# Joining the last score units of two head pairs in one PSUM region, and another rotation of the regions

## The chip, the cores and the metric

The kernel runs on one core of a Trainium2 chip. The metric is the device time of one launch in microseconds (us), the median of five runs. The core's engines are TensorE (PE, matrix multiply; its weight loads are listed as PEld), ScalarE (ACT, activation functions), VectorE (DVE, elementwise), GpSimd (POOL) and SyncE (SP, which issues most of the DMA transfers here). Each engine works through its own queue in order, and waits on semaphores for the others. Matmul results land in PSUM, which has eight banks of 512 float32 columns in 128 partitions.

## The reference

T5 attention with a relative position bias, and behind it a two-layer MLP with the "snake" activation. The eight batches (B = 8, H = 8 heads, S = 576, D = 64) become 4608 tokens of 512.

```python
scores = scale * np.matmul(q, k.transpose(0, 1, 3, 2))
...
scores = scores + bias.transpose(2, 0, 1)[None, :, :, :]
scores = scores - np.max(scores, axis=-1, keepdims=True)
attn = np.exp(scores)
attn = attn / (np.sum(attn, axis=-1, keepdims=True) + 1e-09)
return np.matmul(attn, v).astype(np.float32)
...
h = x @ w_in
s = np.sin(alpha * h)
g = h + s * s / (alpha + 1e-09)
return (g @ w_out).astype(np.float32)
```

## The kernel before

**Attention.** A batch `t` has four pairs of heads, `p` = 0 to 3. The scores of a pair are kept transposed, keys in the partitions, and come in six *units*. Units 0 to 3 are the four chunks of 128 keys against queries 0 to 511: two matmuls of 512 columns, one for each head of the pair, each on 64 rows of the array. The unit `"t"` (tail) is the last 64 keys of both heads against all 576 queries: two matmuls of 288 columns on the full array. Unit 4 is the four key chunks against the last 64 queries: eight matmuls of 64 columns. A unit fills up to two PSUM banks; ACT takes the exponential of a whole unit in one instruction (line 707) and writes it to the SBUF tile `u` of the pair: 1024 elements per partition for units 0 to 3, 576 for the tail, 512 for unit 4. DVE multiplies the part near the diagonal by the exponential of the bias (lines 732 and 715; far from the diagonal the factor is 1). Then PE multiplies `u` by V (`plan_av`, groups of nine matmuls with 128 queries each: three groups for queries 0 to 383, two for the others). The row sums come along as a 65th column, and DVE divides (lines 786 and 787). From batch 1 on, transposing DMAs bring the result to `xT`.

**MLP.** A block `b` is 512 tokens. MLP-in makes 16 *hidden chunks* `f` of 128 columns, four matmuls of 512 columns each (`plan_moe_in`). ACT takes the sine (line 867), ACT or DVE the square (874, 876), DVE makes `g` (881), which frees the chunk's PSUM bank. MLP-out (`plan_mo`) adds 16 matmuls in one bank for each quarter of the block; ACT or DVE copies the result out (538, 540). Exponential and sine are in different activation tables, so ACT loads a table (line 939) between the attention of a batch and the hidden stage behind it, and back.

**PSUM.** Six of the banks are three regions of two banks, `R0`, `R1`, `R2`. A region holds one score unit, or two hidden chunks. Hidden chunk `f` takes `R{f // 2 % 2}`, so the MLP uses R0 and R1 alone and its last chunks, 14 and 15, lie in R1. In batch 0 the attention uses R0 and R1, and the banks of R2 (`ca`, `cb`) serve attention output and transposes; from batch 1 (`LAG - 1`) on, score units rotate over all three regions. The other two banks, `am0` and `am1`, are shared by attention output and MLP-out, whichever is free first. In the last MLP blocks `ca` and `cb` serve MLP-out too.

**The order.** Nothing of it is left to the hardware: `Plan` is a list scheduler that runs when the kernel is built. Each task names its engines with a cost, its dependencies, a priority and its buffers; `Plan.run` picks the task that can start first (the priority decides within 0.02 us) and emits its instructions, which fixes the order in each engine's queue. MLP-out matmuls are *fill* (`fill`): they have the lowest priority, and their number among the scores of a batch is bounded (`QUOTA`). Changes between matmuls on 64 rows and on the full array are charged (`T_MODE`). In `plan_qk` the units are emitted in *groups* of one or two, one PE task each; the exponentials follow in `plan_ex`. Before, two pairs from batch 1 on have seven groups and twelve units, and a unit's region is its place in the batch's sequence modulo three:

```python
((0, 0), (0, 1)), ((0, 2), (0, 3)), ((0, "t"),), ((0, 4), (1, 0)),
((1, 1), (1, 2)), ((1, "t"),), ((1, 3), (1, 4)),
...
r = seq.index(y) % nreg
```

Batch 0's attention comes first, then block 0's hidden stage, then the attention of batches 1 and 2, and from there on a hidden stage (block `t - 1`) behind the attention of each batch; batch 7 is followed by blocks 6, 7 and 8.

Of the kernel before, what the change touches and what calls it, by code (L numbers as in the profile page):

```python
# [24 lines left out]
def t_act(n):  # L25
    return n / 1200.0 + 0.052
# [150 lines left out]
LAG = 2  # L177
# [34 lines left out]
def kernel(  # L212
# [93 lines left out]
    ubs = [sgl.tile([128, 9 * S], F16, name=f"u{i}") for i in range(3)]  # L306
# [40 lines left out]
    def new_sc(r, n):  # L347
        if r not in regs or regs[r][0] != n:
            if r in regs:
                regs.pop(r)[1].release()  # L350
            open_reg(r, n)
        shape = [128, 512] if n == 1 else [128, 2, 512]
        return regs[r][1].tile(shape, F32, name="sc", tag="sc", bufs=3 - n)
# [96 lines left out]
    def full(out, lhsT, rhs, start, stop):  # L450
        nc.tensor.matmul(out=out, lhsT=lhsT, rhs=rhs, start=start, stop=stop)  # L451
# [78 lines left out]
    plan = Plan()  # L530
# [92 lines left out]
    QW = ((0, 512), (512, 64))  # L623

    def plan_qk(t, deps, tails, first, gate, early):

        us, ubs = [Cell() for _ in range(NP)], [Buf("u") for _ in range(NP)]
        dones = [{} for _ in range(NP)]
        if t < LAG - 1:
            groups = [[(p, i)] for p in range(NP) for i in (0, 1, 2, 3, "t", 4)]  # L630
            nreg = 2
        else:
            groups = [
                [(y + p, i) for y, i in g] for p in range(0, NP, 2) for g in (
                    ((0, 0), (0, 1)), ((0, 2), (0, 3)), ((0, "t"),), ((0, 4), (1, 0)),
                    ((1, 1), (1, 2)), ((1, "t"),), ((1, 3), (1, 4)),
                )
            ]
            nreg = 3
        seq = [y for g in groups for y in g]  # L640
        head, exs = qk_last[:], []
        for gi, g in enumerate(groups):
            scs, bufs = [Cell() for _ in g], []
            for y in g:
                r = seq.index(y) % nreg
                bufs.append([Buf(f"R{r}"), Buf(f"R{r}")])

            def qk(e, gi=gi, g=g, scs=scs):
                if gi == 0:
                    first()  # L650
                    plan.in_qk, plan.used = True, 0
                    plan.quota = QUOTA.get(t, QUOTA_ELSE)
                plan.share = (gi + 1) / len(groups)
                if gi == len(groups) - 1:
                    plan.in_qk = False
                kT, qT = kTs[t % 2], qTs[t % 2]
                for (p, i), sc in zip(g, scs):
                    if i == 0:
                        us[p].v = new_u()
                    sc.v = new_sc(seq.index((p, i)) % nreg, 2)  # L660
                    if i == "t":
                        for z in range(2):
                            full(sc.v[:, z, 0:288], kts[t % 2][:, p, :],
                                 qT[:, p, 288 * z : 288 * z + 288], True, True)
                        continue
                    for y in range(1 if i < 4 else 4):
                        q0, n = QW[i == 4]
                        k0 = 128 * (i if i < 4 else y)
                        for z in range(2):
                            r = slice(64 * z, 64 * z + 64)  # L670
                            full(sc.v[:, z, n * y : n * y + n], kT[r, p, k0 : k0 + 128],
                                 qT[r, p, q0 : q0 + n], True, True)

            def base(y):
                k_ = [x for x in seq if x[0] == y[0]].index(y)
                return PB + 100 * (16 * y[0] + 2 * k_)

            dur = sum(0.25 if i == "t" else 0.15 if i == 4 else 0.225 for _, i in g)
            m = plan.add(
                {"PE": dur}, qk,  # L680
                [d for p, i in g for d in deps[p] + (tails[p] if i == "t" else [])],
                min(base(y) for y in g), after=head + early,
                new=[x for y in bufs for x in y] + [ubs[p] for p, i in g if i == 0],
            )
            m.mode = "f" if g[0][1] == "t" else "r"
            head = [m]
            for y, sc, b in zip(g, scs, bufs):
                exs.append(plan_ex(t, y, sc, b, us[y[0]], ubs[y[0]], m, gate, base(y),
                                   dones[y[0]]))
        qk_last[:] = [m]  # L690
        return us, ubs, dones, exs

    def plan_ex(t, y, sc, b, u, ub, m, gate, base, done):

        p, i = y

        def ex(e):
            uz = u.v[:, 0:8, :].rearrange("p (z c) q -> p z c q", z=2)
            if i == "t":
                o = u.v[:, 8, :].rearrange("p (b q) -> p b q", b=2)  # L700
                x = sc.v[:, :, 0:288]
            elif i < 4:
                o, x = uz[:, :, i, 0:512], sc.v
            else:
                o = uz[:, :, :, 512:576]
                x = sc.v[:, :, 0:256].rearrange("p z (c q) -> p z c q", c=4)
            nc.scalar.activation(out=o, in_=x, func=AF.Exp, scale=0.125)  # L707

        n = 576 if i == "t" else 1024 if i < 4 else 512
        x = plan.add({"ACT": t_act(n)}, ex, [m] + gate, base + 20, use=b + [ub])  # L710
        if i == "t":

            def bh(e):
                io = u.v[:, 8, 384:576]
                nc.vector.tensor_tensor(out=io, in0=io, in1=mh[:, p, 0:192], op=ALU.mult)

            done[(0, 4)] = x
            done[(1, 4)] = plan.add({"DVE": 0.19}, bh, [x], base + 10,
                                     nb=0.0 if t else T_MH[p > 0], use=[ub])
            return x  # L720
        w = 0 if i < 4 else 1
        q0, n = QW[w]
        for cc in [i] if i < 4 else range(4):
            done[(w, cc)] = x
            lo, hi = max(q0, 128 * cc - 128), min(q0 + n, 128 * cc + 256)
            if lo >= hi:
                continue

            def bd(e, cc=cc, lo=lo, hi=hi):
                io = u.v[:, 0:8, lo:hi].rearrange("p (z c) q -> p z c q", z=2)[:, :, cc]  # L730
                x0 = lo - 128 * cc + 128
                nc.vector.tensor_tensor(  # L732
                    out=io, in0=io, in1=m2[:, 2 * p : 2 * p + 2, x0 : x0 + hi - lo],
                    op=ALU.mult,
                )

            done[(w, cc)] = plan.add({"DVE": 0.1 + (hi - lo) / 960.0}, bd, [x], base + 10,
                                     nb=0.0 if t else T_M2[p > 0], use=[ub])
        return x
# [103 lines left out]
    def plan_moe_in(b, tbl):  # L843
# [2 lines left out]
        xs012 = [d for w in range(2) for d in xdone[(0, w)][0 : NP - 1]]  # L846
        xs = [d for t in range(T) for w in range(2) for d in xdone.get((t, w), [])
              if S * t + WIN[w][0] < 512 * b + 512 and S * t + sum(WIN[w]) > 512 * b]
        sins = []
        for f in range(NF):  # L850
            hb, sb, qb = Buf(f"R{f // 2 % 2}"), Buf("s16"), Buf("sq")
            h, s16, sq = Cell(), Cell(), Cell()
# [33 lines left out]
            pri = PB + 10000 + 1000 * (b - (PB // 1000000)) + 10 * f  # L886
            if b == 0 and f < 4:
                m = plan.add({"PE": 3 * t_pe(512)}, lambda e, mm=mm: mm(e, range(3)), xs012,
                             pri - 100, nb=T_W, after=qk_last[:], new=[hb])
                m = plan.add({"PE": t_pe(512)}, lambda e, mm=mm: mm(e, range(3, 4)), xs + [m],  # L890
                             pri, use=[hb])
            else:
                m = plan.add({"PE": 4 * t_pe(512)}, mm, xs, pri, after=qk_last[:] + (exps if b == T - 2 else []),
                             new=[hb])
            x = plan.add({"ACT": t_act(512) + 0.09}, sn, [m, al] + tbl, pri, new=[sb], use=[hb])
            y = plan.add({"ACT": t_act(512) + 0.04, "DVE": 0.34}, sqr, [x], pri - 5,
                         new=[qb], use=[sb])
            gdone[(b, f)] = plan.add({"DVE": t_dve(512)}, gg, [y], pri - 6,
                                     after=[gdone[(b, f - 1)]] if f else [],
                                     new=[gbuf[b]] if f == 0 else [],  # L900
                                     use=[hb, qb] if f == 0 else [hb, qb, gbuf[b]])
# [40 lines left out]
    PB = 0  # L942
    tr = {(0, 0, kq): plan_tr(0, 0, kq, -1000, 0.0) for kq in range(2)}
    al = plan_alpha()
    gate, pe_gate, sins, exps = [], [], [], []

    for t in range(T):
        PB = 1000000 * t
# [12 lines left out]
        if 2 <= t < T - 1:  # L961
            aheads[t + 1] = plan.add({"SP": 0.1}, ahead, [], PB - 1000000,
                                     after=avs[t - 1] + xdone[(t - 1, 1)])
# [5 lines left out]
        sins = []  # L969
        deps, tails = [], []  # L970
# [72 lines left out]
```

## Time and profile before

| | us |
|---|---|
| median of 5 runs | 392.88 (391.96 to 393.08) |
| the profiled execution: its time | 393.21 |
| its span in the trace | 391.4 |
| PE busy / ACT busy / DVE busy | 373.8 / 322.9 / 261.4 |
| first scores of batch 1, first of batch 5 | 54.70, 196.36 |
| hidden stage of batch 5, between its two table loads | 217.65 to 235.24 |
| score stage of batch 6 | 235.24 to 257.65 |
| last matmul ends | about 387.6 |

The span runs from the first to the last instruction of the core; the device time holds some 1.8 us more around it. "Busy" counts the time in which an engine has an instruction at work. Matmuls are pipelined: one of 512 columns is listed with 0.38 us though the next starts 0.2155 us after it, so the work of PE is read from start to start. In a timeline a row merges instructions that follow each other, with its first start, its length and, in brackets, the idle time before it and what ended it. The granted clock is the share of TensorE's full clock.

### The profile page before, as it was taken

The numbers are of one execution on the slowest core, as the hardware profiler recorded it, in microseconds if no ns is written. First come the engines' busy times: TensorE is split into PE (matmuls) and PEld (weight loads), VectorE is DVE, ScalarE is ACT, GpSimd is POOL, SyncE is SP. The second block draws the span as 40 slices with busy tenths as digits, with TensorE's granted clock in tenths as the row PEclk, the third lists the DMA queues.
The fourth block names the chain that finished last, engine by engine and source line by source line (L and its number), as shares of the span: only waits on it lengthen the run. The fifth ranks groups of instructions, "written<-read, shape, count | busy, mean of one in ns | idle before, by whom it ended". The sixth has DMA issues, their size and how long they took to land.

```text
span 391.4 us, 8536 instructions
## 1 busy us (share of the span) xinstructions
PE 373.8 (96%) x3381; PEld 187.6 (48%) x3381; DVE 261.4 (67%) x584; ACT 322.9 (82%) x453; POOL 82.0 (21%) x96
## 2 busy tenths in 40 slices
PE   6789979999999999999999999999999999999995
PEld 2356434555544554455445544454455444444442
DVE  3676976776886679568966786679667949429100
ACT  2966998999999999899999999999999959539211
POOL 5664934062630045005300310000000000000000
PEclk9989989999999999999999999999999999999999
DMA  9999999999999999948992298210121000020122
GB/s 169 206 206 220 169 190 167 160 146 129 148 174 155 147 122 159 186 69 92 139 184 57 32 82 171 79 26 13 54 57 47 16 27 28 28 80 2 58 76 80
DMA packets 151207, 42.58 MB, mean 109 GB/s; under 512 B 140344, under 2 KB 145552, under 8 KB 151168
## 3 DMA queue, kind: packets, MB, share of 16 engines
q0 software_dynamic: 89872, 19.04, 60.2%
q1 hardware_dynamic: 61072, 22.95, 32.8%
q8 instruction: 26, 0.43, 0.5%
q14 instruction: 13, 0.11, 0.1%
q10 hardware_dynamic: 224, 0.05, 0.1%
HBM read 37.76 MB, written 16.52 MB: 139 GB/s over the span
## 4 chain that ended last, share of the span: by engine, by line
PE 87%; DMA 4%; DVE 4%; ACT 3%; POOL 1%; issue 1%; ACTq 0%; DVEq 0%
PE sc L451 42%; PE am L451 37%; PE ca L451 4%; PE cb L451 4%; ACT u L707 2%; DMA m2r<-e_dram 2%; DMA e_dram<-e_sb 1%; DMA phi_sb<-phi_const 1%; DVE g L881 1%; DVE u L732 1%; ACT s L867 1%; DVE xn L787 1%; DVE xp L787 0%; DVE rd L786 0%; DVE outs L540 0%
## 5 line engine op out<-in xcount | busy, mean ns | idle before, releaser
L707 ACT ACTIVATE u<-sc 128x1024 f16<-128x1024 f32 (+1 forms) x192 | 157.8, 892 | 15.2 <-PE sc L451 13.5
L451 PE MATMUL sc<-xT,w_in 128*128 128x512 f16 x576 | 132.4, 379 | 0.5 <-DVE g L881 0.5
L881 DVE SCALAR_TENSOR_TENSOR g<-sq,inv_a,sc 128x512 f16<-128x512 f16 x144 | 103.2, 746 | 24.1 <-PE am L451 16.6
L451 PE MATMUL am<-w_out,g 128*128 128x512 f16 x448 | 116.6, 382 | 0.3 <-DVE outs L540 0.2
L867 ACT ACTIVATE s<-sc,alphaT 128x512 f16<-128x512 f32 x144 | 92.9, 678 | 4.7 <-PE sc L451 3.2
L732 DVE TENSOR_TENSOR u<-u,m2r 128x512 f16<-128x512 f16 (+2 forms) x160 | 68.0, 438 | 32.4 <-ACT u L707 30.2
L451 PEld LDWEIGHTS <-w_in 128*128 128x128 f16 x576 | 55.1, 98 | 64.2 <-issue 1.0
L451 PEld LDWEIGHTS <-g 128*128 128x128 f16 x576 | 53.7, 98 | 66.4 <-issue 12.7
L451 PEld LDWEIGHTS <-u 128*128 128x128 f16 x1440 | 55.9, 98 | 20.0 <-issue 9.5
L451 PE MATMUL am<-v,u 128*128 128x65 f16 x1216 | 53.6, 194 | 0.0
L451 PE MATMUL sc<-qT,kT 64*128 64x64 f16 (+1 forms) x512 | 48.7, 294 | 3.4 <-DVE g L881 2.2
L874 ACT ACTIVATE sq<-s 128x512 f16<-128x512 f16 x79 | 49.2, 628 | 2.5 <-DVE g L881 0.8
L397 POOL DMA_DIRECT2D v<-in_v_dram x24 | 21.2, 893 | 115.4 <-PE am L451 114.2
L451 PE MATMUL am<-vh,u 128*128 128x130 f16 x152 | 33.8, 223 | 2.6 <-DVE xp L787 1.3
L876 DVE TENSOR_TENSOR sq<-s 128x512 f16<-128x512 f16 x65 | 27.3, 421 | 5.1 <-ACT s L867 4.4
L787 DVE TENSOR_TENSOR xp<-am,rd 128x384 f16<-128x384 f32 (+1 forms) x56 | 27.5, 491 | 2.0
L451 PEld LDWEIGHTS <-kT 64*128 64x128 f16 x512 | 14.2, 95 | 29.2 <-issue 25.4
L786 DVE RECIPROCAL rd<-am 128x6 f32<-128x6 f32 (+1 forms) x60 | 11.2, 187 | 22.7 <-PE am L451 22.0
L540 DVE COPY outs<-am 128x512 f32<-128x512 f32 x21 | 14.4, 687 | 6.2 <-PE am L451 6.1
L939 ACT ACT_TABLE_LOAD x13 | 16.7, 1283 | 0.2
L378 POOL DMA_DIRECT2D staged_q<-in_q_dram x6 | 15.0, 2495 | 5.6 <-DMA staged_q<-in_q_dram 3.8
L538 ACT ACTIVATE outs<-am 128x512 f32<-128x512 f32 x7 | 4.2, 594 | 13.6 <-PE am L451 13.6
(87 smaller groups left out, 164.7 us busy)
## 6 DMA issues: line engine op xcount, KB each, us to landing
out_dram<-outs SPq DMA_DIRECT2D x36, 256.0 KB, 2.2
staged_k<-in_k_dram POOLq DMA_DIRECT2D x6, 576.0 KB, 16.8
staged_q<-in_q_dram POOLq DMA_DIRECT2D x6, 576.0 KB, 19.9
v<-in_v_dram POOLq DMA_DIRECT2D x24, 128.0 KB, 8.5
w_in<-in_moe_w_in_dram POOLq DMA_DIRECT2D x4, 512.0 KB, 8.6
w_out<-in_moe_w_out_dram POOLq DMA_DIRECT2D x4, 512.0 KB, 17.5
xT<-xp SPq DMA_TRANSPOSE x72, 3.1
w_out<-in_v_dram SPq DMA_DIRECT2D x4, 256.0 KB, 8.0
```

Source lines behind the costliest of these rows:

```text
L378: nc.gpsimd.dma_start(out=dst.ap()[t].rearrange("s (h d) -> s h d", h=H), in_=src[t].rearrange("h s d -> s h d"),)
L397: nc.gpsimd.dma_start(out=vs[t % 2][:, c, :, 0:D], in_=vp[128 * c : 128 * c + 128],)
L451: nc.tensor.matmul(out=out, lhsT=lhsT, rhs=rhs, start=start, stop=stop)
L540: k_of(e).tensor_copy(out=o, in_=i)
L707: nc.scalar.activation(out=o, in_=x, func=AF.Exp, scale=0.125)
L732: nc.vector.tensor_tensor(out=io, in0=io, in1=m2[:, 2 * p : 2 * p + 2, x0 : x0 + hi - lo], op=ALU.mult,)
L787: nc.vector.tensor_tensor(out=y.rearrange("p c (z d) -> p c z d", z=2), in0=a[:, :, :, 0:D], in1=r.unsqueeze(3).to_broadcast([128, nq, 2, ...
L867: nc.scalar.activation(out=s16.v, in_=h.v, func=AF.Sin, scale=alphaT[:, f : f + 1])
L874: nc.scalar.activation(out=sq.v, in_=s16.v, func=AF.Square)
L876: k_of(e).tensor_tensor(out=sq.v, in0=s16.v, in1=s16.v, op=ALU.mult)
L881: nc.vector.scalar_tensor_tensor(out=gcell[b].v[:, f, :], in0=sq.v, scalar=inv_a[:, f : f + 1], in1=h.v, op0=ALU.mult, op1=ALU.add,)
L939: nc.scalar.preload_act_table_set(name)
```

## The change

From batch 1 on, the unit 4 of two neighbouring pairs becomes one unit `"4"`: sixteen matmuls of 64 columns into one region, the second pair's in columns 256 to 511 of each bank. Two exponentials read it, each for its own pair (`x0` is the column offset). Two pairs then have eleven units, a batch 22 instead of 24, and 13 groups instead of 14; the joined unit stands next to a unit of the following pair, or at the end of the batch behind the last key chunk. The region of a unit is no longer its place modulo three but goes through `order`: R2, R0, R1 in turn, in batch 1 R0, R2, R1 and in batch 2 R2, R1, R0. The priorities of the units of a batch are spread evenly over its sequence. The sines and the squares of a hidden stage are each kept in the order of the chunks (`after=`).

```diff
             groups = [
                 [(y + p, i) for y, i in g] for p in range(0, NP, 2) for g in (
-                    ((0, 0), (0, 1)), ((0, 2), (0, 3)), ((0, "t"),), ((0, 4), (1, 0)),
-                    ((1, 1), (1, 2)), ((1, "t"),), ((1, 3), (1, 4)),
+                    (
+                        ((0, 0), (0, 1)), ((0, 2), (0, 3)), ((0, "t"),), ((1, 0), (1, 1)),
+                        ((1, 2), (1, 3)), ((1, "t"),), ((0, "4"), (2, 0)),
+                    ) if p == 0 else (
+                        ((0, 1), (0, 2)), ((0, "t"),), ((0, 3), (1, 0)), ((1, 1), (1, 2)),
+                        ((1, "t"),), ((1, 3), (0, "4")),
+                    )
                 )
             ]
             nreg = 3
+        order = (0, 1) if nreg == 2 else {LAG - 1: (0, 2, 1), LAG: (2, 1, 0)}.get(t, (2, 0, 1))
...
-                r = seq.index(y) % nreg
+                r = order[seq.index(y) % nreg]
...
-                    for y in range(1 if i < 4 else 4):
-                        q0, n = QW[i == 4]
-                        k0 = 128 * (i if i < 4 else y)
+                    s_ = i in (4, "4")
+                    for y in range(8 if i == "4" else 4 if s_ else 1):
+                        q0, n = QW[s_]
+                        k0, p_ = 128 * (y % 4 if s_ else i), p + y // 4
...
-                            full(sc.v[:, z, n * y : n * y + n], kT[r, p, k0 : k0 + 128],
-                                 qT[r, p, q0 : q0 + n], True, True)
+                            full(sc.v[:, z, n * y : n * y + n], kT[r, p_, k0 : k0 + 128],
+                                 qT[r, p_, q0 : q0 + n], True, True)
...
             def base(y):
+                if t >= LAG - 1:
+                    return PB + 100 * (64 * seq.index(y) // len(seq))
...
-                exs.append(plan_ex(t, y, sc, b, us[y[0]], ubs[y[0]], m, gate, base(y),
-                                   dones[y[0]]))
+                for o in range(2 if y[1] == "4" else 1):
+                    p = y[0] + o
+                    exs.append(plan_ex(t, (p, 4) if y[1] == "4" else y, sc, b, us[p], ubs[p], m,
+                                       gate, base(y) + o, dones[p], 256 * o))
...
-                x = sc.v[:, :, 0:256].rearrange("p z (c q) -> p z c q", c=4)
+                x = sc.v[:, :, x0 : x0 + 256].rearrange("p z (c q) -> p z c q", c=4)
...
-            x = plan.add({"ACT": t_act(512) + 0.09}, sn, [m, al] + tbl, pri, new=[sb], use=[hb])
+            x = plan.add({"ACT": t_act(512) + 0.09}, sn, [m, al] + tbl, pri, after=sins[-1:],
+                         new=[sb], use=[hb])
             y = plan.add({"ACT": t_act(512) + 0.04, "DVE": 0.34}, sqr, [x], pri - 5,
-                         new=[qb], use=[sb])
+                         after=sqs[-1:], new=[qb], use=[sb])
+            sqs.append(y)
```

More of the change, by code (lines that the diff above doesn't have):

```diff
@@ L659, in qk @@
                         us[p].v = new_u()
-                    sc.v = new_sc(seq.index((p, i)) % nreg, 2)
+                    sc.v = new_sc(order[seq.index((p, i)) % nreg], 2)
                     if i == "t":
@@ L665, in qk @@
                         continue
-                    for y in range(1 if i < 4 else 4):
-                        q0, n = QW[i == 4]
-                        k0 = 128 * (i if i < 4 else y)
+                    s_ = i in (4, "4")
+                    for y in range(8 if i == "4" else 4 if s_ else 1):
+                        q0, n = QW[s_]
+                        k0, p_ = 128 * (y % 4 if s_ else i), p + y // 4
                         for z in range(2):
                             r = slice(64 * z, 64 * z + 64)
-                            full(sc.v[:, z, n * y : n * y + n], kT[r, p, k0 : k0 + 128],
-                                 qT[r, p, q0 : q0 + n], True, True)
+                            full(sc.v[:, z, n * y : n * y + n], kT[r, p_, k0 : k0 + 128],
+                                 qT[r, p_, q0 : q0 + n], True, True)
             def base(y):
+                if t >= LAG - 1:
+                    return PB + 100 * (64 * seq.index(y) // len(seq))
                 k_ = [x for x in seq if x[0] == y[0]].index(y)
                 return PB + 100 * (16 * y[0] + 2 * k_)
-            dur = sum(0.25 if i == "t" else 0.15 if i == 4 else 0.225 for _, i in g)
+            dur = sum(0.25 if i == "t" else 0.15 if i == 4 else 0.3 if i == "4" else 0.225 for _, i in g)
             m = plan.add(
                 {"PE": dur}, qk,
-                [d for p, i in g for d in deps[p] + (tails[p] if i == "t" else [])],
+                [d for p, i in g for d in deps[p] + (tails[p] if i == "t" else [])
+                 + (deps[p + 1] if i == "4" else [])],
                 min(base(y) for y in g), after=head + early,
@@ L687, in plan_qk, with plan_ex @@
             for y, sc, b in zip(g, scs, bufs):
-                exs.append(plan_ex(t, y, sc, b, us[y[0]], ubs[y[0]], m, gate, base(y),
-                                   dones[y[0]]))
+                for o in range(2 if y[1] == "4" else 1):
+                    p = y[0] + o
+                    exs.append(plan_ex(t, (p, 4) if y[1] == "4" else y, sc, b, us[p], ubs[p], m,
+                                       gate, base(y) + o, dones[p], 256 * o))
         qk_last[:] = [m]
         return us, ubs, dones, exs
-    def plan_ex(t, y, sc, b, u, ub, m, gate, base, done):
+    def plan_ex(t, y, sc, b, u, ub, m, gate, base, done, x0):
         p, i = y
@@ L848, in plan_moe_in @@
               if S * t + WIN[w][0] < 512 * b + 512 and S * t + sum(WIN[w]) > 512 * b]
-        sins = []
+        sins, sqs = [], []
         for f in range(NF):
```

## The prediction

> **What bounds the kernel now.** I read the page first: busy shares, then the chain that ended last.
>
> ```profile
> PE 373.8 (96%) x3381; PEld 187.6 (48%) x3381; DVE 261.4 (67%) x584; ACT 322.9 (82%) x453; POOL 82.0 (21%) x96
> PE 87%; DMA 4%; DVE 4%; ACT 3%; POOL 1%; issue 1%; ACTq 0%; DVEq 0%
> ```
>
> TensorE (PE) is 87% of the chain. Then the stretches: first the start of batch 1, then one hidden stage and one score stage of the steady part (columns: stretch, length, busy time and count of PE, PEld, DVE, ACT, POOL, granted clock, DMA).
>
> ```profile
> 53.24:56.65 3.41, 1.21 (x27) 0.76 (x27) 3.23 (x6) 3.39 (x6) 0.64 (x1) 1.00 1.19 191
> 56.65:60.06 3.41, 3.38 (x11) 0.72 (x11) 0.98 (x2) 2.46 (x4) 0.62 (x1) 0.50 1.21 195
> 217.65:235.24 17.59, 17.59 (x121) 8.79 (x120) 14.47 (x27) 17.19 (x29) 4.79 (x6) 1.00 0.92 67
> 235.24:257.65 22.41, 22.30 (x258) 11.03 (x257) 14.74 (x40) 21.09 (x25) 0.00 (x0) 1.00 0.48 109
> ```
>
> In the steady part PE never rests (17.59 of 17.59, 22.30 of 22.41 us), though ACT waits for scores now and then. So an ACT wait saved there is worth nothing by itself. Only two things can shorten this kernel: less PE work, and fewer PE waits. The timeline of PE shows the work (start, duration, line, operation):
>
> ```profile
> 193.25 3.19 PE L451 MATMUL am<-w_out,g 128*128 128x512 f16 x14
> 196.36 0.61 PE L451 MATMUL sc<-qT,kT 64*128 64x512 f16 x4
> 196.90 1.47 PE L451 MATMUL am<-w_out,g 128*128 128x512 f16 x6
> 198.30 0.61 PE L451 MATMUL sc<-qT,kT 64*128 64x512 f16 x4
> ...
> 201.13 0.51 PE L451 MATMUL sc<-qT,kT 64*128 64x64 f16 x10
> 201.57 0.39 PE L451 MATMUL am<-w_out,g 128*128 128x512 f16 x1
> ```
>
> Read start to start. A 512-column matmul takes 0.2155 us (20 MLP-in matmuls from 221.91 to 226.22). 14 of them are 3.02, and the score block comes after 3.11: 0.09 extra; 6 are 1.29 and take 1.40: 0.11. The block of two units takes 0.54 for 2 x 0.2155 (the two 64-row matmuls of a unit run together): 0.11 more. So **each block of 64-row score matmuls costs about 0.20 us** besides its work, 0.10 entering and 0.10 leaving. The block at 201.13 (one unit and a short unit of eight 64-column matmuls) takes 0.44, so the eight are 0.44 - 0.216 - 0.11 = 0.115.
>
> The waits of PE that I could find after 53 us:
>
> ```profile
> 54.70 0.39 PE L451 MATMUL sc<-qT,kT 64*128 64x512 f16 x2 [0.64 <-DVE g L881]
> 56.67 0.61 PE L451 MATMUL sc<-qT,kT 64*128 64x512 f16 x2 [1.59 <-DVE g L881]
> 57.22 1.89 PE L451 MATMUL am<-w_out,g 128*128 128x512 f16 x4
> ...
> 95.37 0.38 PE L451 MATMUL am<-w_out,g 128*128 128x512 f16 x1
> 96.17 0.23 PE L451 MATMUL am<-vh,u 128*128 128x130 f16 x1 [0.42 <-DVE xp L787]
> ...
> 102.75 4.58 PE L451 MATMUL sc<-xT,w_in 128*128 128x512 f16 x20 [0.31 <-DVE g L881]
> ...
> 124.93 0.59 PE L451 MATMUL am<-w_out,g 128*128 128x512 f16 x2 [0.18 <-DVE outs L540]
> ```
>
> At the start of batch 1 the second score unit waits for the last hidden chunk's g. Next come four matmuls at half clock, 0.46 us each. At 95.37 one output matmul (0.216) leaves 0.58 lost until 96.17: the attention output needs the bank that DVE still normalizes.
>
> **The change part by part.** I took the instruction order of both builds.
>
> *Fewer blocks.* From batch 1 on, each batch has 9 blocks of 64-row matmuls where it had 10 (63 against 70 over seven batches), with the same matmuls in them. 7 x 0.20 = **-1.4**. The ends are 6 x 0.18 and 8 x 0.22 (1.1 to 1.8). Sixteen short matmuls in a row are priced at the rate of eight, 0.23; were weight loads not to keep up, each would take its load of 0.095 (the 64-row load row of the page) in pairs, 0.02 more for each of 16 pairs a batch, +2.2 at most; I take 0, as the eight show no slowing.
>
> [...]
>
> *Start of batch 1.* Before, from 54.70 to 62.22 PE did five score units (1.08), one short unit (0.12), a tail (0.24), eight output matmuls (1.73) and three block switches (0.6): 3.77 of work in 7.52, so 3.75 lost. After, the second unit goes to R2 and waits only for the qT copy out of bank cb, which DVE ends at 55.97, not for g at 56.62. But then ACT paces: exponentials follow each other at 0.91 (a long and a short one take 1.51, the short 0.60) from 56.81, a region is free 1.05 after its exponential starts, and the order lets few output matmuls in. Following it I get waits of 1.1, 0.6, 0.4, 0.6, 0.2, 0.5 and 0.2 = 3.6. **-0.2**; ends -1.5 (none of the waits after the first two) and +0.8 (the half clock as well).
>
> The half clock follows the stretch in which PE was busy 1.21 of 3.41 us; the stretch from 60.06, busy 3.10 of 3.41, stays at full clock. [...] By the rows the new stretch holds 1.21 + 0.5 us of work, and I let the clock stay up.
>
> *Banks am0 and am1.* The attention output finds its bank busy when the last user ended less than 1.04 us of PE work earlier (0.46 + 0.58 at 95.37). Before that happens three times (95, 174, 294 us), after twice: **-0.6**. Two output groups that waited for a copy (0.35 at 124.6, 0.27 at 244.1) have more than 1.05 us between now: **-0.6**. But in the last stage two output groups follow each other on am1 with nothing between: a copy on ACT takes 0.60 and starts 0.38 after the last matmul starts, less the 0.22 that this matmul takes: **+0.8**; PE keeps its order, so the five output matmuls behind it and the last two hidden stages are late by as much.
>
> *Hidden stages (batches 2 to 7).* The wait of 0.47 at 102.75 (chunk 4 of batch 2, its region's g late on DVE) goes: two attention groups and four output matmuls now stand ahead of that chunk. **-0.5**. In exchange two short exponentials now end the attention, so the table load comes 0.5 later after the last score block (2.45, was 217.65 - 215.69 = 1.96) while PE starts hidden chunks at the same distance. ACT and DVE then both need 1.82 us for two chunks (ACT two sines and a square; DVE 0.42 + 2 x 0.70), PE 1.73 plus what is mixed in. A chunk needs the region of the chunk four before. Following batch 5 with these, its stage now without an output copy on ACT (0.58), chunk 15 comes 16.65 after the last score block and chunk 11's g ends at 16.35; the other margins are 0.05 to 0.35. I take 0.15 per stage, **+0.9**; ends 0 and 0.6 per stage (3.6).
>
> *First score group of a batch.* It stands 4 output matmuls (0.86) behind the last hidden chunk, not 12 to 14. It needs R2, free, and R0, whose chunk 13 has its g 0.4 to 0.75 after the last hidden matmul (193.25 to 193.99 in batch 4). Cover 0.86 + 0.10: **0**; if ACT runs 0.5 late, +0.3 each, 1.8. The first exponential then starts with the table loaded; the 0.16 to 0.63 that ACT waited there is ACT's alone: 0. The keys are there: the last load of a batch's keys is issued 14 us or more before its first group (100.67 and 116.55 in batch 3).
>
> *Other edits.* The order forced on sines and squares follows nearly the order of before: 0. Batch 2 ends with its fourth key unit on R0, so chunks 2 and 3 run first and the first sine starts 0.5 late; DVE hides it in the margins above: 0, at most +0.5.
>
> Sum: -1.4 - 0.2 - 0.6 - 0.6 + 0.8 - 0.5 + 0.9 = **-1.6**. The span goes from 391.4 to 389.8. The profiled execution took 393.21, 0.33 over the median of 392.88; I take 1.6 off the median: **391.3**.
>
> **Rivals.**
> *It is given back.* DVE and ACT are 1.82 against PE's 1.73 in the hidden stages; the 2.5 gained elsewhere only lets PE arrive sooner at a region that isn't free. Against it: the margins above. 0.4 per stage x 6 = 2.4, so **392.8**, no change (within 0.2% is what a measurement of this kernel can tell from none).
> *Slower: the hidden stages become DVE's.* The place is chunks 4 to 15, the price is the lead lost: 0.49 (the second short exponential) + 0.35 (PE reaches chunk 15 at 16.65, was 17.0) = 0.84 in each of six stages, 5.0 less 2.5: **395.4**. It decides from 0.42 per stage. For it: margins before of only 0.17 and 0.34 at 231.83 and 232.70. Against it: the copy that leaves ACT there.
> *The start of batch 1 pays in full.* No half clock and ACT without its wait of 0.94 at 59.69: 1.5 more, **389.8**.
> *The change doesn't free the start:* the first group still takes R0, so it waits for chunk 13 where it waited for chunk 15; in the steady part neither was a wait of PE, which is why I count 0 there.
>
> **Numbers.** Forecast 0.45, range of its own 390.4 to 392.4; batch 1 in full 0.13; given back 0.24; slower 0.18. Faster by over 0.2% means under 392.1: 0.13 + 0.43 of the forecast's, 0.56; within: 0.24 + 0.02 = 0.26; slower 0.18. The range, 389.2 to 394.2, leaves out most of the slower case.
>
> **What would show it.** Nine blocks a batch, 0.20 each, in PE's timeline. No half clock at 56 to 60. First exponential right behind each table load, and PE none the faster for it. One wait of 0.8 on am1 in the last stage. I am wrong if PE waits for DVE g by more than 0.4 in each hidden stage.

## The result and the profile after

| | before | after |
|---|---|---|
| median (lowest to highest) | 392.49 us (44 runs) | 390.45 us (389.44 to 392.04, 25 runs) |
| ratio after : before | | 0.9952, 95% interval 0.994 to 0.9965 |
| profiled execution: time, span | 393.21, 391.4 | 389.98, 388.2 |
| first scores of batch 1 | 54.70 | 53.62 |
| from there to the end of the span | 336.70 | 334.58 |

The change gains 0.48%, 1.9 us by this ratio and 2.0 by the medians. Up to the first scores of batch 1 both kernels run the same instructions in the same order. In the profiled executions of this study that point lies anywhere between 53.4 and 55.8 us, so spans are compared from there on: -2.12. Ten of the changed kernel's 25 executions took 391.25 to 392.04 us and the others 389.44 to 390.98; a late start alone can do that, as one execution of e6 below shows (391.91, first scores at 55.84), so kernels that lie within 1.5 us of each other are compared by their spans.

The page of the changed kernel, its busy times and its chain of waits by engine:

```profile
PE 373.5 (96%) x3381; PEld 186.5 (48%) x3381; DVE 263.4 (68%) x588; ACT 319.1 (82%) x449; POOL 82.1 (21%) x96
PE 89%; ACT 6%; DMA 1%; issue 1%; DVE 1%; ACTq 0%; DVEq 0%
```

TensorE has the same 3381 matmuls and a larger share of the chain. ACT has four instructions fewer: four squares that DVE now does. The last chain goes less over DVE (4% before, 1% now) and more over ACT (3% before, 6% now), and less of PE's waiting ends with DVE and more of it with an exponential, as the timelines below show.

Four stretches of the changed kernel (length, busy time and count of PE, PEld, DVE, ACT, POOL, granted clock, DMA): two at the start of batch 1, then the hidden stage of batch 5 and the score stage of batch 6, each from one table load to the next.

```profile
51.86:55.27 3.41, 1.83 (x31) 0.85 (x29) 3.26 (x6) 3.39 (x6) 1.36 (x2) 1.00 1.23 190
55.27:58.69 3.42, 3.42 (x13) 1.08 (x12) 1.32 (x4) 3.41 (x5) 0.61 (x1) 0.50 1.22 196
...
210.31:227.13 16.82, 16.82 (x134) 8.44 (x131) 15.21 (x30) 16.41 (x26) 4.79 (x6) 1.00 0.82 57
227.13:249.04 21.91, 21.91 (x245) 11.03 (x244) 15.09 (x38) 20.74 (x26) 0.00 (x0) 1.00 0.50 125
```

In the steady part PE still never rests by its listed durations (16.82 of 16.82, 21.91 of 21.91). The half clock is still there at the start of batch 1 (0.50 in the second row), where I had said it would be gone.

PE's timeline after: the start of batch 1, chunk 4 of batch 2's hidden stage, a tail in batch 4, the joined unit in batch 5, and the last MLP stage (start, duration, operation, in brackets the idle time before it and what ended it).

```profile
53.62 0.39 PE L451 MATMUL sc<-qT,kT 64*128 64x512 f16 x2 [0.64 <-DVE g L893]
54.95 0.39 PE L451 MATMUL sc<-qT,kT 64*128 64x512 f16 x2 [0.93 <-DVE qT L540]
55.27 1.46 PE L451 MATMUL am<-w_out,g 128*128 128x512 f16 x3
56.66 1.04 PE L451 MATMUL sc<-qT,kT 64*128 64x512 f16 x4
57.63 0.61 PE L451 MATMUL am<-w_out,g 128*128 128x512 f16 x1
...
102.25 0.38 PE L451 MATMUL am<-w_out,g 128*128 128x512 f16 x1
102.46 4.52 PE L451 MATMUL sc<-xT,w_in 128*128 128x512 f16 x20
...
167.16 0.39 PE L451 MATMUL am<-w_out,g 128*128 128x512 f16 x1
167.67 0.41 PE L451 MATMUL sc<-qT,kt 128*128 128x288 f16 x2
...
196.94 1.89 PE L451 MATMUL am<-w_out,g 128*128 128x512 f16 x8
198.76 0.62 PE L451 MATMUL sc<-qT,kT 64*128 64x64 f16 x18
199.32 0.23 PE L451 MATMUL am<-vh,u 128*128 128x130 f16 x1
...
318.47 0.81 PE L451 MATMUL am<-w_out,g 128*128 128x512 f16 x3 [0.69 <-ACT outs L538]
```

The second score unit now comes 1.33 after the first, not 1.97, and it is qT that releases it, as said. The wait at chunk 4 (0.31 listed, 0.47 from the starts) is gone: 102.25 to 102.46 is one matmul's 0.2155. At 198.76 stands the joined unit with a unit of the next pair behind it: 0.56 = 0.216 + 16 x 0.0147 + 0.11, so the short matmuls run at the rate of the eight before. At 167.16 one output matmul takes 0.51: the tail behind it waited 0.295 for its region. At 318.47 is the forecast wait on am1 (0.69 listed, 0.85 from the starts).

Waits like the one behind 167.16 are easy to miss (there are two of 0.295 and four of 0.056): a short idle behind a listed duration of 0.38 shows only when the starts are subtracted.

### The profile page after: what moved, and what is told of

Read it like the earlier page. It is cut to its first block, busy times and chain, and to the rows that moved or that the text cites. A ratio compares the mean times of both kernels' runs of the same rounds, so it can differ in the third digit from the quotient of the medians.

```text
span 388.2 us, 8498 instructions
## 1 busy us (share of the span) xinstructions
PE 373.5 (96%) x3381; PEld 186.5 (48%) x3381; DVE 263.4 (68%) x588; ACT 319.1 (82%) x449; POOL 82.1 (21%) x96
## 4 chain that ended last, share of the span: by engine, by line
PE 89%; ACT 6%; DMA 1%; issue 1%; DVE 1%; ACTq 0%; DVEq 0%
PE sc L451 43%; PE am L451 37%; PE ca L451 4%; ACT u L719 4%; PE cb L451 4%; DMA phi_sb<-phi_const 1%; ACT s L879 1%; PE cb L560 1%; PE am L560 1%; DVE kT L540 0%; ACT L953 0%; ACT outs L538 0%; ACT sq L886 0%; DVE xp L799 0%; DVE g L893 0%
## 5 line engine op out<-in xcount | busy, mean ns | idle before, releaser
L719 ACT ACTIVATE u<-sc 128x1024 f16<-128x1024 f32 (+1 forms) x192 | 155.6, 897 | 8.5 <-PE sc L451 7.4
L451 PEld LDWEIGHTS <-g 128*128 128x128 f16 x576 | 53.5, 98 | 67.8 <-issue 15.1
L886 ACT ACTIVATE sq<-s 128x512 f16<-128x512 f16 x75 | 46.6, 630 | 2.3 <-DVE g L893 0.5
L888 DVE TENSOR_TENSOR sq<-s 128x512 f16<-128x512 f16 x69 | 28.9, 420 | 6.6 <-ACT s L879 6.3
```

Of the source, the lines that this page charges most:

```text
L886: nc.scalar.activation(out=sq.v, in_=s16.v, func=AF.Square)
L888: k_of(e).tensor_tensor(out=sq.v, in0=s16.v, in1=s16.v, op=ALU.mult)
```

## The experiments

All are read by one account. From the first scores of batch 1 to the end of the span, the time should be PE's work (324.65 with 70 blocks, 323.32 with 63, from the start-to-start times), plus PE's waits summed the same way (a start is late against the rate at full clock, 0.2155 for a matmul of 512 columns where the half clock gave 0.46, so the time lost to a half clock is in them), plus a constant of some 5 us for the drain at the end and what is too small to list.

| kernel | median, ratio to before (95%) | first scores to end | PE's waits in it | stretch of batches 1, 2 | ACT idle in that stretch |
|---|---|---|---|---|---|
| before | 392.49 | 336.70 | 6.88 | 42.62 | 2.55 |
| before, run again (e8) | 392.33, 0.9988 (0.9975 to 1.0002) | 335.90 | 6.07 | 41.78 | 1.61 |
| after | 390.45, 0.9952 (0.994 to 0.9965) | 334.58 | 6.26 | 39.61 | 0.57 |
| e1 without the new turn | 392.24, 0.9998 (0.998 to 1.0016) | 336.66 | 8.30 | 42.66 | 3.49 |
| e2 new turn alone | 394.25, 1.0057 (1.0045 to 1.0069) | 338.56 | 8.60 | 43.17 | 2.10 |
| e9 old priorities | 392.40, 0.999 (0.9975 to 1.0004) | 336.54 | 8.27 | 42.42 | 3.35 |
| e3 other first bank | 389.31, 0.993 (0.9915 to 0.9944) | 333.60 | 5.16 | 39.61 | 0.57 |
| e5 begins and ends on R1 | 389.19, 0.9917 (0.9903 to 0.9931) | 333.00 | 4.65 | 39.61 | 0.56 |
| e6 old turn from batch 3 | 389.79, 0.9937 (0.9914 to 0.9961) | 334.26 | 5.95 | 39.61 | |
| e7 sines unforced | 389.31, 0.9921 (0.9904 to 0.9939) | 333.62 | 5.26 | 39.61 | |
| e4 42 more switches | 399.21, 1.0182 (1.0164 to 1.02) | 343.18 | 4.70 | | |

Each row has one profiled execution. "ACT idle" adds the waits for scores that the timeline lists, those over some 0.15. "Stretch of batches 1, 2" runs from the first scores of batch 1 to the first hidden chunk of the stage behind batch 2. It holds 64 output matmuls in before, e1, e2 and e9, and 56 in the others of 39.61; the eight (1.73) are done later there, so the stretch alone is not the gain. Work plus waits plus 4.95 to 5.3 gives the third column in every row but e4, which needs its own work (below).

e8, the kernel before once more, was expected to start batch 1 between 53.5 and 55 and to take 336.7 within 0.3 from there on. It started at 53.90 and took 335.90, so the second half of that was missed: this execution had no half clock at the start of batch 1 (granted 1.00 from 48.21 to 58.45), and its stretch of batches 1 and 2 is 0.84 shorter.

**e1 and e2: the change without the new turn, and the new turn alone.** e1 keeps the joined units, the even priorities and the forced order of sines and squares, and puts the regions back in their old turn.

```diff
-        order = (0, 1) if nreg == 2 else {LAG - 1: (0, 2, 1), LAG: (2, 1, 0)}.get(t, (2, 0, 1))
+        order = (0, 1, 2)
```

> The changed kernel with the regions in their old turn (place in the sequence modulo three). The order of instructions has 63 blocks of 64-row score matmuls as after the change, the first score group of batches 4 to 7 stands 9 to 13 output matmuls behind the last hidden chunk again, and on the two shared banks it has one attention group too close behind another (0.6 us), two output groups slightly too close (0.2 each) and none on am1 in the last stage. Theory (PE work and waits alone count): the 1.4 us of the fewer blocks stay, the bank waits are 0.8 less than after the change, the start of batch 1 loses 0.6 because its second unit waits for the last hidden chunk again: 390.0 to 390.6, as fast as the whole change. Rival (the rotation brings the gain, since ACT starts its exponentials sooner): 391.8 or more.

Measured 392.24: no gain at all, so the expectation failed. The 63 blocks are there, and what they save is given back as waits, 8.30 against 6.88. PE's timeline of e1:

```profile
53.84 0.39 PE L451 MATMUL sc<-qT,kT 64*128 64x512 f16 x2 [0.64 <-DVE g L893]
55.82 0.58 PE L451 MATMUL sc<-qT,kT 64*128 64x512 f16 x2 [1.59 <-DVE g L893]
...
102.97 1.02 PE L451 MATMUL sc<-xT,w_in 128*128 128x512 f16 x4 [0.75 <-DVE g L893]
```

The second unit waits for the last g of the hidden stage again, and in batch 2's hidden stage a chunk waits 0.75 (0.91 from the starts) for the region of the chunk four before it.

e2 is the kernel before with only the new `order` line (and the two uses of it); the units stay apart and the priorities are the old ones.

> The kernel before with the new turn of the regions alone, units not joined: 70 blocks, the first score group 4 output matmuls behind the last hidden chunk. Its order has three attention groups closer than 0.7 us behind another in their bank, five output groups 0.65 to 0.84 behind one, and one output group right behind another on am1. Theory: no gain from blocks, about 2 us more of bank waits than before the change, 0.6 less at the start of batch 1: 393.0 to 394.5, no faster than before. Rival (the rotation brings the gain): 390.5 to 391.3.

Measured 394.25, in the range of the theory; its sum is another. The waits on the two shared banks grew from 2.4 to 3.6, by 1.2 and not by 2, and there is a wait of 1.0 that it doesn't name, in front of the first hidden chunk behind batch 2:

```profile
95.70 0.51 PE L451 MATMUL sc<-qT,kT 64*128 64x512 f16 x10
97.21 1.02 PE L451 MATMUL sc<-xT,w_in 128*128 128x512 f16 x4 [1.00 <-ACT u L708]
```

With 24 units a batch the new turn ends batch 2 in the region that the first hidden chunk needs, and the chunk waits for the exponential. So the new turn alone loses, and the change without it gains nothing; only together do they gain.

**e6 and e5: where the turn matters.** Both are the changed kernel with another turn from batch 3 on: e6 that of before, `.get(t, (0, 1, 2))`, which begins and ends a batch on R0; e5 one that begins and ends on R1, `.get(t, (1, 0, 2))`. The builder then puts more output matmuls ahead of the first scores (13 in batch 5 of e5 where the changed kernel has 4).

> The changed kernel with the turn R0, R1, R2 from batch 3 on (batches 1 and 2 as changed). Attention then begins and ends on R0, which the hidden stage needs first. Theory: the joined unit holds R0 until its second exponential is done, so PE waits 0.2 us before the hidden chunks of most batches, as with the old turn throughout; the bank waits are 0.3 less than after the change: 390.6 to 391.3. With the old turn throughout (392.2) the rest, 1 us or more, was then lost in batches 1 and 2. Rival (the loss there came from batches 3 to 7): 392.0 or more.

> The changed kernel with the turn R1, R0, R2 from batch 3 on (batches 1 and 2 as changed): attention begins on R1, which holds the last hidden chunks, and ends on R1, which the hidden stage needs only for its third chunk. The first score group of a batch stands 13 to 15 output matmuls behind the last hidden chunk again. Theory (PE's waits count, and beginning on a free region is only ACT's gain): as the changed kernel, less the 0.85 us of am1, which this order doesn't have: 389.4 to 389.9. Rival (beginning on a region that the MLP doesn't use is what pays): 391.3 or more.

e5 gave 389.19 and e6 389.79, both below the ranges expected for them. e6 is not slower than the changed kernel, so e1's loss comes from the turn in batches 1 and 2 (its waits there, in the hidden stage behind them and at the first scores after that). In the steady part it is worth nothing to begin on the region that the MLP leaves free, which is what the prediction's zero for the first score group said. What e5 gains over the change is an order without the wait on am1 (0.85), and with one tail wait of 0.295 where the change has two; the other 0.4 are smaller waits. By its span it is the fastest of the study (333.00 against 334.58 for the change), though in their medians e3 and e7 lie within 0.12 of it.

**e3: the wait on am1 alone.** The first late output group takes the other bank.

```diff
-    its = {"avE": 0, "moE": 0, "moL": 0}
+    its = {"avE": 0, "moE": 0, "moL": 1}
```

> The changed kernel with the three banks of the last output groups taken in the turn ca, cb, am1 instead of am1, ca, cb; the order of all instructions stays. Theory: the one wait of 0.85 us of PE on am1 in the last stage goes and nothing takes its place: 0.7 to 0.9 faster than the changed kernel, 389.6. Rival (that stage is paced by something else, so the wait is given back): 390.4.

Measured 389.31; the median is 1.1 under the changed kernel's, more than the 0.7 to 0.9 expected, but the span gives 0.98. The wait of 0.85 is gone and no other stage changed by over 0.05 us: the last stage, from its first hidden chunk to the end of the span, went from 101.37 to 100.52. In this profiled execution the clock stayed up at the start of batch 1 (granted 1.00 from 50.84 to 61.08), and all seven waits that the prediction had followed by hand stand in the trace: 1.10, 0.55, 0.37, 0.62, 0.23, 0.44, 0.23 (predicted 1.1, 0.6, 0.4, 0.6, 0.2, 0.5, 0.2). e5, with the same first stages, shows who ends them:

```profile
54.30 0.39 PE L451 MATMUL sc<-qT,kT 64*128 64x512 f16 x2 [0.64 <-DVE g L893]
55.62 0.39 PE L451 MATMUL sc<-qT,kT 64*128 64x512 f16 x2 [0.94 <-DVE qT L540]
55.95 0.82 PE L451 MATMUL am<-w_out,g 128*128 128x512 f16 x3
56.70 0.39 PE L451 MATMUL sc<-qT,kT 64*128 64x512 f16 x2
57.49 0.39 PE L451 MATMUL sc<-qT,kT 64*128 64x512 f16 x2 [0.40 <-ACT u L719]
57.82 0.39 PE L451 MATMUL am<-w_out,g 128*128 128x512 f16 x1
58.41 0.40 PE L451 MATMUL sc<-qT,kt 128*128 128x288 f16 x2 [0.20 <-ACT u L719]
58.65 0.81 PE L451 MATMUL am<-w_out,g 128*128 128x512 f16 x3
```

Behind the first two units it is always ACT. The three output matmuls at 55.95 take 0.75 to the next start here and 1.39 in the changed kernel's own profile (55.27 to 56.66), at half clock. Still the stretch is 39.61 in both: at half clock PE worked through what it otherwise waited.

**e4: the price of a block.** A matmul of 64 columns on the full array stands between the two units of 42 score groups, and makes 105 blocks of 63.

```diff
+                    if t >= LAG - 1 and len(g) == 2 and (p, i) == g[1] and i in (1, 2, 3):
+                        full(sc.v[:, 0, 0:64], zz[:, 0:128], zz[:, 0:64], True, True)
```

> The changed kernel with one full-array matmul of 64 columns between the two units of 42 score groups (its result is overwritten), the order of all else kept: 105 blocks instead of 63. Theory: each split costs one way out and one way in, 0.19, and the matmul 0.03: 42 x 0.22 = 9.2 us slower than the changed kernel, 399.7. Rival (a switch is hidden under the neighbouring matmuls, and only the start-to-start distance shows it): 42 x 0.03 = 1.3 slower, 391.7.

Measured 399.21, 8.8 over the changed kernel. One of the 42 places in PE's timeline:

```profile
197.53 0.39 PE L451 MATMUL sc<-qT,kT 64*128 64x512 f16 x2
197.85 0.20 PE L451 MATMUL sc<-zz 128*128 128x64 f16 x1
197.99 0.39 PE L451 MATMUL sc<-qT,kT 64*128 64x512 f16 x2
198.31 0.39 PE L451 MATMUL am<-w_out,g 128*128 128x512 f16 x1
```

A unit that was followed by the next after 0.216 is followed by the extra matmul after 0.32, and that takes 0.14: 0.24 for each place, of which some 0.03 to 0.04 is the matmul itself (an estimate: 512 columns take 0.2155, and an attention group of nine matmuls with 650 columns 0.30). 42 x 0.24 = 10.1, less the waits that it filled (6.26 - 4.70 = 1.56) = 8.5; the stretch from the first scores to the end grew by 8.6. So about 0.20 a block was paid at full wherever PE had no wait to hide it in.

**e7: the forced order of sines and squares.** The changed kernel without `after=` on them.

> The changed kernel without the forced order of sines and squares. Theory: the order did nothing for PE; this order of instructions has no output group right behind another on am1 (-0.85) and two small bank waits of 0.2 more: 389.6 to 390.3. Rival (without it a hidden stage waits for its chunks out of turn): 391.3 or more.

Measured 389.31. This is just under the range. The forced order brings PE nothing; without it the builder's order happens to have no wait on am1, and 0.85 of the 0.96 by which its span is shorter is that.

**e9: the priorities.** The changed kernel without the even spread of priorities, which the prediction did not price.

```diff
-                if t >= LAG - 1:
-                    return PB + 100 * (64 * seq.index(y) // len(seq))
```

> The changed kernel, but the units of a batch keep the priorities of before (16 a pair, 2 a unit) where the change spreads them evenly. Blocks of 64-row matmuls stay 63, regions turn as in the change; only the mixing of output matmuls and attention groups between the scores is another. My account (work of PE plus its waits) has no term for the priorities: 389.9 to 391.2, as the changed kernel within 0.6. Rival: the even spread is what keeps ACT supplied in batches 1 and 2; then the stretch from the first scores of batch 1 to the first hidden chunk of the stage behind batch 2, 39.61 us in the changed kernel, grows to over 41 and the time is 391.8 or more.

Measured 392.40: the rival's time. ACT's timeline in the stretch of batches 1 and 2, e9 first, then the changed kernel (in brackets how long it waited for scores):

```profile
67.96 2.48 ACT L717 ACTIVATE u<-sc 128x1024 f16<-128x1024 f32 x3 [0.32 <-PE sc L451]
70.62 4.32 ACT L717 ACTIVATE u<-sc 128x1024 f16<-128x1024 f32 x5 [0.18 <-PE sc L451]
75.30 2.00 ACT L717 ACTIVATE u<-sc 128x512 f16<-128x512 f32 x3 [0.36 <-PE sc L451]
77.83 1.94 ACT L717 ACTIVATE u<-sc 128x1024 f16<-128x1024 f32 x2 [0.53 <-PE sc L451]
80.68 2.48 ACT L717 ACTIVATE u<-sc 128x1024 f16<-128x1024 f32 x3 [0.90 <-PE sc L451]
```

```profile
55.74 12.92 ACT L719 ACTIVATE u<-sc 128x1024 f16<-128x1024 f32 x16
68.85 23.88 ACT L719 ACTIVATE u<-sc 128x1024 f16<-128x1024 f32 x29 [0.19 <-PE sc L451]
93.11 2.00 ACT L719 ACTIVATE u<-sc 128x1024 f16<-128x1024 f32 x3 [0.38 <-PE sc L451]
```

With the even spread ACT runs 29 exponentials without a listed wait; without it, it waits eight times. e9 then ends batch 2 as e1 does: a hidden chunk of it waits 0.78 for its region, and the waits of PE sum to 8.27. My expectation named the priorities as no term of the account and missed that they decide the waits.

Not all of the 8.27 need be the priorities'. Four output matmuls of e9, at 56.85, 60.26, 63.59 and 67.00, each start 0.04 to 0.05 us after a quarter of `w_out` has landed, and their waits add up to 1.03. One of them is long enough to be listed:

```profile
63.59 0.38 PE L451 MATMUL am<-w_out,g 128*128 128x512 f16 x1 [0.21 <-DMA w_out<-in_moe_w_out_dram]
```

The first quarter landed 1.75 us after the first scores in this execution (56.81) and 0.53 after them in the changed kernel's (54.15), and it is the slowest of e9's ten (393.40). That e9 loses the gain rests on its median; how much of its stretch of 42.42 comes from the late weights stays open.

**e10 and e11: who paces batches 1 and 2.** The tail's exponential of pair 1 in batch 1 is done three times, in the changed kernel (e10) and in the one before (e11).

```diff
-            nc.scalar.activation(out=o, in_=x, func=AF.Exp, scale=0.125)
+            for _ in range(3 if y == (1, "t") and t == LAG - 1 else 1): nc.scalar.activation(out=o, in_=x, func=AF.Exp, scale=0.125)
```

> The changed kernel, with the exponential of the tail unit of pair 1 in batch 1 done three times over (the same values): two more ACT instructions of 128x576, some 0.6 us each, early in the stretch of batches 1 and 2; the order on PE is that of the changed kernel. Theory: in the changed kernel ACT paces this stretch (it idles only 0.19 and 0.38 us in it), so its 39.61 us become 40.3 to 40.8. Rival: PE paces it, and ACT's work is cover: 39.6 to 39.9.

> The kernel before, with the same two more exponentials in batch 1. Theory: there ACT waits for scores six times in the stretch (1.6 us behind the start of batch 1), PE paces, so the stretch of 41.78 us without the half clock (42.62 with it) grows by at most 0.5: 41.8 to 42.3, or 42.6 to 43.1 with the half clock. Rival: both kernels are alike in this and it grows by 0.7 to 1.2 here too.

Both missed, and e11 as its rival had it; each was executed once, so only their stretches are compared. The two instructions cost ACT 1.36 (13 exponentials in 10.42 became 15 in 11.78). The stretch grew by 1.07 in the kernel before (41.78 to 42.85), so at the start of batch 1 ACT sets PE's pace there too, and the theory that it does so only after the change falls. e11's ACT timeline has 24 exponentials without a listed wait:

```profile
55.53 19.20 ACT L707 ACTIVATE u<-sc 128x1024 f16<-128x1024 f32 x24
```

In the changed kernel the stretch grew by 2.90 (39.61 to 42.51), more than the work added. Its timeline and its stretches show where:

```profile
63.82 0.39 PE L451 MATMUL sc<-qT,kT 64*128 64x512 f16 x2 [0.28 <-ACT u L719]
65.73 0.23 PE L451 MATMUL am<-vh,u 128*128 128x130 f16 x1 [1.52 <-ACT u L719]
```

```profile
62.49:65.90 3.41, 1.61 (x27) 0.68 (x25) 1.54 (x4) 3.35 (x6) 2.60 (x2) 1.00 1.60 141
65.90:69.31 3.41, 3.41 (x34) 1.74 (x32) 1.51 (x6) 2.10 (x4) 0.97 (x1) 0.50 1.61 162
```

PE's wait for ACT that ends at 65.73 grew from 0.23 to 1.59, which is the 1.36. Its stretch, with PE busy 1.61 of 3.41, is followed by another 3.41 us at half clock, in which ACT was busy for 2.10 alone: it waited 1.31 for scores. The other 1.5 are lost there; that the half clock alone costs them is argued from these rows, as no run has the longer wait without it.

## Why the prediction was right

The time was 390.45 where 391.3 was forecast. Of the 0.85 between them 0.39 is the starting point, a median of 392.88 from 5 runs that is 392.49 from 44; the gain was 2.0 instead of 1.6. In time the result lies nearer to the rival in which the start of batch 1 pays in full (389.8), but that start gave 0.24 and not 1.7, so it is the forecast's case that held, with two terms mis-sized. By its own steps, from the two traces:

| step | predicted | measured |
|---|---|---|
| seven blocks fewer | -1.4 | -1.33 (seven times 0.19, from the starts) |
| start of batch 1 | -0.2 | -0.24 (waits 3.80 before, 3.56 after) |
| attention's bank | -0.6 | -0.88 (three of 0.585, now two of 0.44) |
| output groups behind a copy | -0.6 | -0.62 |
| am1 in the last stage | +0.8 | +0.85 |
| chunk 4 of batch 2 | -0.5 | -0.53 |
| new waits in six hidden stages | +0.9 | 0 |
| tail units that wait for an exponential | none | +0.8 (two of 0.295, four of 0.056) |
| sum, with two waits of 0.1 that came and went | -1.6 | -2.0 (the spans: -2.1) |

The blocks are the part that lasts. Against the run of the kernel before in which the clock stayed up (e8: 335.90, waits 6.07) the changed kernel gains 1.32, the blocks' 1.33, and its waits, 6.26, are no fewer. e4 shows the same price from the other side.

The step that failed is "I take 0.15 per stage, +0.9". The stage itself had been followed rightly: in batch 5 chunk 15 was to come 16.65 after the last score block with chunk 11's g ending at 16.35, and the trace has 16.69 (207.86 to 224.55) and 16.40 (224.26). The margin of 0.29 held, no hidden stage behind batches 3 to 7 has a wait, and the 0.15 was a reserve for stages that I had not followed. The rival in which the hidden stages become DVE's falls with it: DVE is busy 15.21 of 16.82 there.

The waits that did come are in the score stages, at tails whose region still holds an exponential being read. I had followed the regions through the hidden stages only. In their sum the two errors nearly cancel (0.9 against 0.8), which is luck, and the remaining 0.3 to 0.5 is the bank that the attention waits for, whose waits became shorter as well as fewer.

"I let the clock stay up" was wrong for the profiled execution, though the stretch held 1.83 us of work where 1.71 was foreseen, and it made no difference: 39.61 with the half clock (0.50 from 55.27 to 58.69) and without it (e3, e5). In the kernel before it does: 42.62 with it, 41.78 in e8 without. There PE falls behind ACT (ACT's wait of 0.94 at 59.69 is missing in e8); after the change the second unit comes 0.65 earlier and ACT has exponentials waiting throughout.

The sign that the first exponential stands right behind each table load came true too: 0.01 us behind it at all six loads from batch 1 on, where before it was up to 0.63. PE is none the faster for it: in e5 and e6, which begin on a region of the MLP from batch 3 on, ACT waits up to 0.86 there, and they are not slower.

What the prediction left out is the priorities. It read the order that they lead to and so priced them unknowingly, but it could not have said that without them the change gains nothing (e9). e1 shows that the joined units and the spread gain nothing without the turn, and e9 that the joined units and the turn gain nothing without the spread; turn and spread without the joined units were not run. Why the even spread keeps ACT supplied, beyond the fact that it does, was not tried apart from the order as a whole.

## What to carry to other kernels

Where one engine is busy throughout, count its switches and its waits separately: the switches saved here were paid out in full (0.20 us each), while the waits moved from one resource to the next and are best followed resource by resource, region and bank alike, through every stage. Before calling one part of a change the cause, run it without each part; here the whole gains 0.5%, and taking out the turn or the even priorities brings the gain to nothing. Subtract starts, not listed durations, when looking for waits, and look past the first scores that all variants share, since the part before them moved by over 2 us from run to run.

## What the runs showed of the hardware

The half clock at the start of batch 1 comes and goes between kernels that run the same instructions up to there. It is in the profiled executions of before (granted 0.50 from 56.65 to 60.06), after (0.50 from 55.27 to 58.69), e10 (0.55 over 55.30 to 58.70) and e1 (four output matmuls of 512 columns in 1.89, as in before). It is not in those of e3 (1.00 from 50.84 to 61.08), e8 (1.00 from 48.21 to 58.45), e11 (1.00 from 50.32 to 60.56), e5 (three output matmuls that take 0.75 to the next start, 1.39 in after) and e7 (a mean of 1.0 over the whole execution).

In the traces of before and after all changes of the clock lie a whole number of 3.413 us apart: at 25.93, 29.34, 56.65, 60.06 and 391.16 in the one, at 7.49, 21.14, 55.27, 58.69 and 386.37 in the other (60.06 to 391.16 is 97 times 3.413). In stretches of that length, the one ahead of the half clock at the start of batch 1 has PE busy 35% of its time before (1.21 of 3.41) and 54% after (1.83 of 3.41), and the one ahead of e10's second half clock 47% (1.61 of 3.41). In executions without a half clock there, the stretch in which the wait falls has 57% in e3 (1.95 of 3.42), 59% in e8 (2.02 of 3.41) and 53% in e11 (1.82 of 3.41). Earlier in before, 59% (2.01 of 3.41 from 22.52 on) was followed by 0.50. That it depends on where the wait falls on the grid, which the start moves from run to run (first scores at 53.62 to 55.84), is my estimate from these rows (e3's wait is split over two stretches, with 1.95 and 2.60 of work); no run tries it alone.

```profile
50.84:54.25 3.41, 2.92 (x35) 1.50 (x34) 3.05 (x6) 3.30 (x7) 0.89 (x2) 1.00 1.30 199
54.25:57.67 3.42, 1.95 (x11) 0.59 (x10) 2.18 (x5) 3.39 (x5) 0.63 (x1) 1.00 1.21 195
57.67:61.08 3.41, 2.60 (x18) 0.91 (x18) 2.08 (x5) 3.41 (x5) 0.61 (x1) 1.00 1.22 197
```

At the end of e11, whose mean granted clock is 1.0, a stretch of 1.60 of 3.42 is followed by the full clock too:

```profile
384.82:388.24 3.42, 1.60 (x8) 0.52 (x6) 0.00 (x0) 0.60 (x1) 0.00 (x0) 1.00 0.19 74
388.24:391.00 2.76, 0.00 (x0) 0.00 (x0) 0.00 (x0) 0.00 (x0) 0.00 (x0) 1.00 0.16 58
```

e10's 1.61 led to the half clock and e11's 1.60 did not, so I give no threshold.
